# First step of an attention and two-MoE kernel: per-head scans of s, constant rows by GpSimd, two row loads for the fourth pair, idle matmuls on a constant tile

## The chip, the cores and the metric

The kernel runs on one core of a Trainium2 chip. The metric is the device time of one execution in microseconds (us); of several executions the median is given. A core has five engines with a queue each: TensorE (PE in the profile), VectorE (DVE), ScalarE (ACT), GpSimd (POOL) and SyncE (SP), which here issues DMAs. Each engine works its queue in order and waits on semaphores for the others.

## The reference

Causal attention with a bias from running sums of s, then two expert-like layers, all in one launch. Shapes: q, k, v of 4 batches, 8 heads, 576 positions, 64 dimensions; s of 4 x 8 x 576.

```python
scores = scale * np.matmul(q, k.transpose(0, 1, 3, 2))       # scale = 1/8
cum = np.cumsum(np.maximum(s, 0.0), axis=-1)
bias = -(cum[:, :, :, None] - cum[:, :, None, :])
scores = np.where(causal, -1e9, scores + np.minimum(bias, 0.0))
attn = softmax(scores); out = np.matmul(attn, v)
x = out as 2304 tokens x 512
h = np.maximum(np.maximum(x @ w1, x @ w2), x @ w3); x = h @ w_out        # d_ff 768
y = ((x @ w_a) * (x @ w_b)) @ w_out2                                     # d_ff 1536
```

## The kernel before, in words

Heads go in pairs: 4 batches by 4 pairs of two heads. The sums of s are never subtracted on a vector engine: they enter the scores through extra rows of the contraction. Where a pair's 64 rows of k and q end, two more rows hold a sum and a constant, so that the matmul adds cum of the key and takes off cum of the query; the factor 8 (the root of 64) in them cancels the scale. For most of the kernel these operands come ready-made from DRAM (tiles of 66 rows), with the sums written to DRAM first (`store_sums`, L194 on) and loaded back.

The first step is different, and the change lies in it alone. `lead_in()` (L1069) does the first 256 positions (Q0 = 256) of batch 0 for all four pairs p = 0 to 3 before the sums have been through DRAM. s is loaded with one partition for each pair of batch and pair (16 partitions), its columns being the two heads by 256 positions, and it is loaded four times, to partitions 64 to 127 (L173). Tiles `cum` and `sraw` hold the sums and s. A pair's operand tiles (`kraw` for p = 0, 1 and `kqv` for p = 2, 3, one tile for k and q) get k and q in partitions 0 to 63 by one DMA each (`lead_load`, L482). Partitions 64 to 127 are filled on the chip: k gets ones times a column of the identity in 64 to 95, which selects the row of pair p, and the sums times such a column in 96 to 127 (L1080, L1086); q gets the negative sums times 8 in 64 to 95 and the constant 8 in 96 to 127 (L1084, L1090). The scores of the first step are then matmuls with 128 rows of contraction (L1114), whose 64 upper rows are zero but for the pair's own.

Behind the scores of a head (`fs`, two matmuls of 128 and 256 columns) come the softmax in two parts: `sm_a` (L594), the masked minimum on VectorE (L608) and the exponential on ScalarE (L615), and `sm_b` (L621), the reciprocal on VectorE and the normalisation on GpSimd (L629). The normalised scores are transposed on TensorE (`ts`, L720), copied to SBUF by ScalarE or VectorE (L723) and multiplied with v (`pv`, L747), and the result is split into a high and a low part (Xh, Xl). The masked scores stand in tiles `F0` with the tag "P", of which there are four. `w_next` converts the first expert weights into high and low parts (hg and lg) between these steps; the gate matmuls (L813) use them.

Before the first scores, `spin` (L154) runs ten idle matmuls on the identity. A further one stands between the last pairs.

What sets the order: a scheduler puts each engine's instructions in a row by priority (`tc.high_priority`, higher first), by readiness and by `tc.issue_after`, which ties an instruction behind another. In `lead_in` the loads and idle matmuls have 5000, the rows of sums 4900, the loads of v and weights 4800, the rest 4000; the scan of s has 5100. SyncE issues nearly all loads in one queue: s, the four pairs' k and q, the tail of s, v, and then five weight loads of 512 KB.

## Time and profile before

| | |
|---|---|
| median of 3 runs | 882.74 us (882.62 to 883.32) |
| the profiled execution | 882.94 us |
| its span in the profile | 881.1 us |
| busy: TensorE, VectorE, ScalarE, GpSimd | 99%, 72%, 46%, 23% of the span |

The profile is one execution as the hardware's profiler recorded it. The times in its rows count from the start of the span, and the execution's own time has 1.84 us more around the span. Two records stand for one fp32 matmul of the program, so ten idle matmuls are 20 records. Busy shares are a mean over stages with different limits; what a change in one stage does is read from that stage's rows, and above all from what each engine waits for there. A row's last bracket gives the engine's idle time before the instruction and what ended it.

### The profile page before, as it was taken

The numbers are of one execution on the slowest core, as the hardware profiler recorded it, in microseconds if no ns is written. First come the engines' busy times: TensorE is split into PE (matmuls) and PEld (weight loads), VectorE is DVE, ScalarE is ACT, GpSimd is POOL, SyncE is SP. The second block draws the span as 40 slices with busy tenths as digits, with TensorE's granted clock in tenths as the row PEclk, the third lists the DMA queues.
The fourth block names the chain that finished last, engine by engine and source line by source line (L and its number), as shares of the span: only waits on it lengthen the run. The fifth ranks groups of instructions, "written<-read, shape, count | busy, mean of one in ns | idle before, by whom it ended". The sixth has DMA issues, their size and how long they took to land.

```text
span 881.1 us, 16779 instructions
## 1 busy us (share of the span) xinstructions
PE 869.9 (99%) x6024; PEld 828.0 (94%) x6024; DVE 633.9 (72%) x1437; ACT 402.0 (46%) x872; POOL 202.2 (23%) x316
## 2 busy tenths in 40 slices
PE   8999999999999999999999999999999999999998
PEld 6777999889999998999999999999999999999998
DVE  7986556675777666765797867777776859987873
ACT  7685745575656645554564323232322224433321
POOL 5324322233423323200003111111111310322210
PEclk9999999999999999999999999999999999999999
DMA  7665644265234763383302134444442353354331
GB/s 228 195 203 175 162 119 138 80 172 155 66 98 115 242 188 123 127 297 132 131 1 73 37 120 141 159 141 159 141 158 94 110 185 124 97 169 134 96 120 49
DMA packets 68291, 120.10 MB, mean 136 GB/s; under 512 B 6944, under 2 KB 50672, under 8 KB 68208
## 3 DMA queue, kind: packets, MB, share of 16 engines
q1 hardware_dynamic: 61016, 111.63, 39.9%
q10 hardware_dynamic: 7192, 7.40, 2.5%
q8 instruction: 48, 0.79, 0.4%
q14 instruction: 35, 0.29, 0.1%
HBM read 87.99 MB, written 31.01 MB: 135 GB/s over the span
## 4 chain that ended last, share of the span: by engine, by line
PE 94%; DMA 1%; DVE 1%; ACT 1%; issue 1%; POOL 1%; ACTq 0%; POOLq 0%; DVEq 0%
PE X L1270 29%; PE g L813 25%; PE Z L1270 15%; PE Y L1270 8%; PE fpv L747 5%; PE t L765 3%; PE f L681 2%; PE s L637 2%; PE s L638 2%; DMA wraw<-in_moe_w_dram 1%; PE ft L720 1%; PE W L1270 1%; PE sj L671 1%; PE tj L778 1%; PE sj L672 1%
## 5 line engine op out<-in xcount | busy, mean ns | idle before, releaser
L813 PE MATMUL g<-Xh,hg 128*128 128x256 f32 (+1 forms) x576 | 175.1, 307 | 1.3 <-ACT hg L81 0.6
L813 PE MATMUL g<-Xh,lg 128*128 128x256 f32 (+1 forms) x576 | 172.5, 301 | 0.3 <-DVE lg L92 0.3
L813 PE MATMUL g<-Xl,hg 128*128 128x256 f32 (+1 forms) x576 | 172.8, 301 | 0.0
L813 PEld LDWEIGHTS g<-Xh,hg 128*128 128x128 f32 x576 | 108.3, 189 | 5.6 <-ACT hg L81 1.2
L813 PEld LDWEIGHTS g<-Xh,lg 128*128 128x128 f32 x576 | 108.6, 189 | 3.0 <-DVE lg L92 1.3
L813 PEld LDWEIGHTS g<-Xl,hg 128*128 128x128 f32 x576 | 108.8, 189 | 1.8 <-issue 0.7
L88 POOL TENSOR_SCALAR wh<-wval 128x256 fp32r<-128x256 f32 x77 | 41.0, 542 | 273.4 <-DVE wval L346 224.2
L1270 PE MATMUL X<-xh,wh 128*128 128x384 f32 x288 | 97.2, 338 | 0.0
L1270 PE MATMUL X<-xl,wh 128*128 128x384 f32 x288 | 96.9, 336 | 0.0
L1270 PE MATMUL X<-xh,wl 128*128 128x384 f32 x288 | 96.9, 337 | 0.0
L1270 PE MATMUL X<-woh,slot 128*128 128x256 f32 x408 | 76.6, 281 | 0.5 <-ACT ob L1317 0.5
L629 POOL TENSOR_SCALAR P<-P,rs 128x128 f32<-128x128 f32 (+2 forms) x80 | 50.3, 634 | 96.2 <-DVE rs L625 70.2
L359 DVE TENSOR_TENSOR slot<-hraw,slot 128x768 fp32r<-128x768 f32 x60 | 60.9, 1041 | 13.7 <-POOL slot L88 11.0
L359 DVE TENSOR_TENSOR u<-Z,u 128x384 f32<-128x384 f32 x72 | 39.6, 552 | 37.9 <-ACT u L1317 28.2
L1270 PEld LDWEIGHTS X<-woh,slot 128*128 128x128 f32 x408 | 64.3, 189 | 0.7 <-ACT ob L1317 0.7
L615 ACT ACTIVATE P<-P,nm 128x128 f32<-128x128 f32 (+2 forms) x80 | 46.6, 583 | 34.6 <-DVE nm L608 26.1
L822 DVE TENSOR_TENSOR hf<-g,hf 128x256 f32<-128x256 f32 (+1 forms) x96 | 43.6, 454 | 24.7 <-PE g L813 18.6
L1270 PE MATMUL X<-wol,slot 128*128 128x256 f32 x204 | 56.9, 280 | 0.0
L81 ACT ACTIVATE slot<-hraw 128x768 fp32r<-128x768 f32 x39 | 32.5, 845 | 52.5 <-DVE hraw L359 25.9
L1270 PEld LDWEIGHTS X<-xh,wh 128*128 128x128 f32 x288 | 54.1, 188 | 0.5 <-DVE u L359 0.3
L1270 PEld LDWEIGHTS X<-xl,wh 128*128 128x128 f32 x288 | 54.1, 188 | 0.0
L1270 PEld LDWEIGHTS X<-xh,wl 128*128 128x128 f32 x288 | 54.0, 188 | 0.0
(214 smaller groups left out, 2208.8 us busy)
## 6 DMA issues: line engine op xcount, KB each, us to landing
hT<-u SPq DMA_DIRECT2D x72, 192.0 KB
hraw<-hT SPq DMA_DIRECT2D x36, 384.0 KB
wraw<-in_moe_w_dram SPq DMA_DIRECT2D x18, 512.0 KB
wraw<-in_moe_w_out_dram SPq DMA_DIRECT2D x18, 512.0 KB
kraw<-in_kT_dram SPq DMA_DIRECT2D x24, 288.0 KB
wraw<-in_moe_w_a_dram SPq DMA_DIRECT2D x12, 512.0 KB
wraw<-in_moe_w_b_dram SPq DMA_DIRECT2D x12, 512.0 KB
st<-h1T SPq DMA_DIRECT2D x24, 192.0 KB
```

What stands on the lines that cost most here:

```text
L81: return nc.scalar.activation(o, i, AF.Copy, scale=scale)
L88: nc.gpsimd.tensor_scalar(o, i, scale, 1.0, op0=ALU.mult, op1=ALU.mult)
L359: return {"V": nc.vector, "P": nc.gpsimd}[e].tensor_tensor(o, a, b, op=op)
L615: e_ = nc.scalar.activation(pt[:, c0:c1], pt[:, c0:c1], AF.Exp, bias=first, scale=-1.0, accum_out=sm[:, g : g + 1],)
L629: n_ = nc.gpsimd.tensor_scalar(pt[:, c0:c1], pt[:, c0:c1], rs[:, g : g + 1], 1.0, op0=ALU.mult, op1=ALU.mult,)
L637: nc.tensor.matmul(ps, QA1[:, qs], KB1[:, h, ksl], start=True, stop=False)
L638: nc.tensor.matmul(ps, QA2[:, qs], KB2[:, h, ksl], start=False, stop=True)
L747: e_ = nc.tensor.matmul(ps[h * D : h * D + D, c0:n], w, x, start=(t == 0), stop=(t == len(mm[h]) - 1),)
L765: nc.tensor.transpose(ps[:, j * P : j * P + P], pt[:, j * P : j * P + P], ident)
L813: nc.tensor.matmul(ps[:, :n], w[:, kk, :], x[:, kk, :], start=(i == 0), stop=(i == len(mm) - 1),)
L822: st["V"] = nc.vector.tensor_tensor(hf, ps[:, :n], hf, op=ALU.max)
L1270: e_ = nc.tensor.matmul(ps[:, :n], w, x, start=(first and i == 0), stop=(i == len(mm) - 1), skip_group_check=not first,)
```

## The change

- Scan: s is clipped and scanned by halves of 256 columns, one head each. VectorE clips the first half, ScalarE the second. The tile `reset`, which restarted the single scan at the second head, is gone. `scan_half(1)` is tied behind the first k sums of pair 0.
- Sums and constants: pair 0's rows of sums are made by halves. The constant rows of q for pairs 0 to 2 become memsets on GpSimd; the sums of k for pairs 1 and 2 and of q for pair 2 are GpSimd's, the sums of q for pairs 0 and 1 ScalarE's. A one-column exponential stands first on ScalarE.
- Fourth pair: no rows of 64 to 127. Two rows (64 and 65) of k and q are set to -8 and 8 by GpSimd and one of each is overwritten by a DMA from partition 67 of `cum`, and its matmuls contract over 66 rows.
- Idle matmuls: eleven, on a constant tile of ones, which exists before the kernel's own code. The identity gets the highest priority; the mask's tile is cleared by VectorE instead of GpSimd.
- Score tiles: both heads of the third pair use tag "sv", the first head of the fourth uses the tile that `reset` had; five heads share the four buffers of tag "P".

```diff
@@ -112,11 +112,12 @@
 
 
     ident = const.tile([P, P], F32, name="ident")
-    make_identity(nc, ident)
+    with tc.high_priority(5200):
+        make_identity(nc, ident)
 
     maskJ = const.tile([P, S // 2 + 4 * P], BF16, name="maskJ")
     mask = maskJ[:, S // 2 :]
-    nc.gpsimd.memset(maskJ, 0.0)
+    nc.vector.memset(maskJ, 0.0)
     nc.gpsimd.affine_select(
         out=mask[:, 3 * P :], in_=mask[:, 3 * P :], compare_op=ALU.is_ge, fill=NEG,
         base=0, pattern=[[-1, P]], channel_multiplier=1,
@@ -154,9 +155,10 @@
     def spin(n):
 
         ps = ps_m.tile([P, 512], F32, tag="m", name="spin")
+        one = nc.const_aps.tensor(1.0, [P, P], F32)
         for _ in range(n):
             last_pe[:] = [
-                nc.tensor.matmul(ps[:, :P], ident, ident, start=True, stop=True).ins
+                nc.tensor.matmul(ps[:, :P], one, one, start=True, stop=True).ins
             ]
 
     last_pe = [None]
@@ -167,18 +169,24 @@
         return ap_.tile([P, w], dt, tag=nm, bufs=1, name=f"e{nm}")
 
     cum, sraw = early("KB1"), early("KB2")
-    reset, ones = early("QA1")[:, : 2 * Q0], early("QA2")[:, : 2 * Q0]
+    ones = early("QA2")[:, : 2 * Q0]
     up, rr = slice(64, P), slice(64, 64 + SR)
+    halves = [slice(0, Q0), slice(Q0, 2 * Q0)]
     with tc.high_priority(5100):
         for a, e in enumerate((nc.sync, nc.scalar, nc.sync, nc.scalar)):
             e.dma_start(sraw[64 + a * SR : 64 + (a + 1) * SR, : 2 * Q0], s[:, : 2 * Q0])
-        nc.vector.memset(reset[up], 1.0)
-        nc.vector.memset(reset[up, Q0 : Q0 + 1], 0.0)
+        nc.scalar.activation(
+            ap_.tile([P, 1], F32, tag="small", bufs=10, name="warm"),
+            nc.const_aps.tensor(0.0, [P, 1], F32), AF.Exp,
+        )
         nc.vector.memset(ones[up], 1.0)
-        nc.vector.tensor_scalar_max(sraw[up, : 2 * Q0], sraw[up, : 2 * Q0], 0.0)
+        nc.vector.tensor_scalar_max(sraw[up, :Q0], sraw[up, :Q0], 0.0)
+        nc.scalar.activation(sraw[up, Q0 : 2 * Q0], sraw[up, Q0 : 2 * Q0], AF.Relu)
+
+    def scan_half(h):
+        c = halves[h]
         nc.vector.tensor_tensor_scan(
-            cum[up, : 2 * Q0], reset[up], sraw[up, : 2 * Q0], 0.0,
-            op0=ALU.mult, op1=ALU.add,
+            cum[up, c], ones[up, :Q0], sraw[up, c], 0.0, op0=ALU.mult, op1=ALU.add,
         )
 
     def scan_tails():
@@ -1071,29 +1079,52 @@
         LP = range(NP)
         with tc.high_priority(5000):
             lead = [lead_load(p) for p in LP]
-            spin(10)
+            spin(11)
         with tc.high_priority(4900):
             kk = [kn for kn, qn, vn in lead]
             qq = [qn for kn, qn, vn in lead]
             lo_, hi_r = slice(64, 96), slice(96, P)
-            for p in LP:
+
+            def k_sums(e, p, c):
+                return e.tensor_scalar(
+                    kk[p][hi_r, c], cum[hi_r, c], ident[hi_r, 96 + p : 97 + p], 1.0,
+                    op0=ALU.mult, op1=ALU.mult,
+                )
+
+            def q_sums(p, c):
+                nc.scalar.activation(
+                    qq[p][lo_, c], cum[lo_, c], AF.Copy, scale=-float(D) ** 0.5
+                )
+
+            for p in range(3):
                 (nc.vector if p < 2 else nc.gpsimd).tensor_scalar(
                     kk[p][lo_], ones[lo_], ident[lo_, 64 + p : 65 + p], 1.0,
                     op0=ALU.mult, op1=ALU.mult,
                 )
-                nc.scalar.activation(qq[p][hi_r], ones[hi_r], AF.Copy, scale=float(D) ** 0.5)
-            for p in LP:
-                (nc.vector if p < 2 else nc.gpsimd).tensor_scalar(
-                    kk[p][hi_r], cum[hi_r, : 2 * Q0], ident[hi_r, 96 + p : 97 + p], 1.0,
-                    op0=ALU.mult, op1=ALU.mult,
-                )
-                nc.scalar.activation(
-                    qq[p][lo_], cum[lo_, : 2 * Q0], AF.Copy, scale=-float(D) ** 0.5
-                )
+                nc.gpsimd.memset(qq[p][hi_r], float(D) ** 0.5)
+            nc.gpsimd.memset(kk[3][64:66], -float(D) ** 0.5)
+            nc.gpsimd.memset(qq[3][64:66], float(D) ** 0.5)
+            scan_half(0)
+            k_ = k_sums(nc.vector, 0, halves[0])
+            q_sums(0, halves[0])
+            with tc.issue_after(k_.ins):
+                scan_half(1)
+            k_sums(nc.vector, 0, halves[1])
+            q_sums(0, halves[1])
+            for p in (1, 2):
+                k_sums(nc.gpsimd, p, slice(0, 2 * Q0))
+            q_sums(1, slice(0, 2 * Q0))
+            nc.gpsimd.tensor_scalar(
+                qq[2][lo_], cum[lo_, : 2 * Q0], -float(D) ** 0.5, 1.0,
+                op0=ALU.mult, op1=ALU.mult,
+            )
         with tc.high_priority(4800):
             nc.sync.dma_start(sraw[rr, 2 * Q0 :], s[0:SR, 2 * Q0 :])
             for p in LP:
                 nc.sync.dma_start(lead[p][2], qv0[0, p][:, 2 * Q0 :])
+            row = cum[67:68, : 2 * Q0]
+            nc.sync.dma_start(kk[3][64:65], row)
+            nc.sync.dma_start(qq[3][65:66], row)
             for j in range(NL):
                 fetch_w1(w1_keys[j])
 
@@ -1107,13 +1138,19 @@
             for h in range(2):
                 pool, tag = (ps_m, "m") if h else (ps_s, "s")
                 ps = pool.tile([P, 512], F32, tag=tag, name="f0")
-                pt = ap_.tile([P, S], F32, tag="P", bufs=4, name="F0")
+                if p == 2:
+                    pt = ap_.tile([P, 5 * P], F32, tag="sv", bufs=2, name="F0")
+                elif (p, h) == (3, 0):
+                    pt = early("QA1")
+                else:
+                    pt = ap_.tile([P, S], F32, tag="P", bufs=4, name="F0")
                 for i in range(2):
                     o = ps[:, P * i : P * (2 * i + 1)]
+                    kr = P if p < 3 else 66
                     def mm(o=o, i=i):
                         last_pe[:] = [nc.tensor.matmul(
-                            o, two(qq[p])[:, h, i * P : i * P + P],
-                            two(kk[p])[:, h, 0 : P * (i + 1)], start=True, stop=True,
+                            o, two(qq[p])[:kr, h, i * P : i * P + P],
+                            two(kk[p])[:kr, h, 0 : P * (i + 1)], start=True, stop=True,
                         ).ins]
                     on_pe(mm)
                 pend.append(sm_a([[(ps[:, 0:P], 0)], [(ps[:, P : 3 * P], P)]], pt, SCALE))
```

What it does to the rows of two engines at the start, and to TensorE's at the end of the first step. First GpSimd, from its first instruction of the kernel to the first normalisation (kraw: pairs 0 and 1; kqv: pairs 2 and 3; eKB_115: the sums; eQA: the ones). Before:

```order
masks.py:197 MEMSET ident 128x128
L119 MEMSET maskJ 128x800
masks.py:199 ISA
masks.py:199 AFFINE_SELECT ident<-ident 128x128
L120 AFFINE_SELECT maskJ<-maskJ 128x128
L126 AFFINE_SELECT maskJ<-maskJ 64x64 x2
L1080 TENSOR_SCALAR kqv<-eQA_118,ident 32x512 x2
L1086 TENSOR_SCALAR kqv<-eKB_115,ident 32x512 x2
L629 TENSOR_SCALAR F_217<-F_217,rs 128x128
```

After, from behind the identity's memset and two constant rows of L1104 on:

```order
masks.py:199 ISA
masks.py:199 AFFINE_SELECT ident<-ident 128x128
L1104 MEMSET kraw 32x512
L1100 TENSOR_SCALAR kqv<-eQA_117,ident 32x512
L121 AFFINE_SELECT maskJ<-maskJ 128x128
L127 AFFINE_SELECT maskJ<-maskJ 64x64 x2
L1105 MEMSET kqv 2x512
L1106 MEMSET kqv 2x512
L1089 TENSOR_SCALAR kraw<-eKB_115,ident 32x512
L1089 TENSOR_SCALAR kqv<-eKB_115,ident 32x512
L1117 TENSOR_SCALAR kqv<-eKB_115 32x512
L637 TENSOR_SCALAR F_221<-F_221,rs 128x128
```

Constant rows (L1104), the setting of the fourth pair's rows (L1105, L1106) and the sums of pairs 1 and 2 (L1089, L1117) stand there now; the mask's clearing has left, and the constants and sums of the fourth pair too.

SyncE, from the tail of s to the first store of sums (eKB_116: s; wraw: the expert weights). Before:

```order
L1094 DMA eKB_116<-in_s_dram 16x640
L1096 DMA qvraw<-in_qv_dram 128x256 x2
L1096 DMA kqv<-in_qv_dram 128x256 x2
L247 DMA wraw<-in_moe_w_dram 128x1024 x5
L196 DMA ck<-eKB_115 32x1x256
L498 DMA kraw<-in_k_dram 64x1152
```

After:

```order
L1122 DMA eKB_116<-in_s_dram 16x640
L1124 DMA qvraw<-in_qv_dram 128x256 x2
L1124 DMA kqv<-in_qv_dram 128x256 x2
L1126 DMA kqv<-eKB_115 1x16x32
L1127 DMA kqv<-eKB_115 1x16x32
L255 DMA wraw<-in_moe_w_dram 128x1024 x5
L204 DMA ck<-eKB_115 32x1x256
L205 DMA ck<-eKB_115 32x1x320
```

The two row loads of the fourth pair have come between the loads of v (qvraw, kqv) and of the weights, and wait for the second scan half and GpSimd's memset of their rows.

TensorE, at the end of the first step, from the last product with v to the first gates (fj: joint scores of the last 64 positions of two heads; hg, lg: high and low part of the gate weights). Before:

```order
L747 MATMUL fpv<-PF,kqv 64x256 x2
L747 MATMUL fpv<-PF,kqv 64x128 x2
L681 MATMUL fj<-kraw,qvraw 64x288 x4
L813 MATMUL g<-Xh,hg_0_140 128x256
L813 MATMUL g<-Xl,hg_0_140 128x256
L813 MATMUL g<-Xh,lg_0_141 128x256
L813 MATMUL g<-Xh,hg_0_140 128x256
```

After:

```order
L755 MATMUL fpv<-PF,kqv 64x128 x2
L821 MATMUL g<-Xh,hg_0_139 128x256
L821 MATMUL g<-Xl,hg_0_139 128x256
L821 MATMUL g<-Xh,lg_0_140 128x256
L821 MATMUL g<-Xh,hg_0_139 128x256
L821 MATMUL g<-Xl,hg_0_139 128x256
L821 MATMUL g<-Xh,lg_0_140 128x256
L821 MATMUL g<-Xh,hg_0_139 128x256
L821 MATMUL g<-Xl,hg_0_139 128x256
L821 MATMUL g<-Xh,lg_0_140 128x256
L821 MATMUL g<-Xh,hg_0_139 128x256
L689 MATMUL fj<-kraw,qvraw 64x288 x4
```

The joint scores stood ahead of the first gate matmul; now ten gate matmuls stand ahead of them, three of which use lg.

## Rows read from the trace of the kernel before

**Rows 1.** The page, section 4: share of the chain that ended last, by engine.
```profile
PE 94%; DMA 1%; DVE 1%; ACT 1%; issue 1%; POOL 1%; ACTq 0%; POOLq 0%; DVEq 0%
```

**Rows 2.** Stretches (start:end, length, busy us and count by engine, PEclk, DMA).
```profile
10.00:13.00 3.00, 2.64 (x17) 1.90 (x15) 2.84 (x12) 2.20 (x10) 1.49 (x4) 1.00 1.02 404
...
25.00:30.00 5.00, 4.23 (x28) 3.31 (x27) 5.00 (x12) 1.41 (x3) 2.18 (x3) 1.00 0.58 192
...
60.00:80.00 20.00, 19.43 (x133) 14.28 (x132) 16.14 (x47) 14.23 (x31) 9.08 (x15) 1.00 0.66 196
...
100.00:200.00 100.00, 99.89 (x774) 93.93 (x773) 61.22 (x202) 59.72 (x155) 27.85 (x50) 1.00 0.50 141
```

**Rows 3.** The chain that ended last, first 30 us (start, length, what).
```profile
1.20 2.05 DMA eKB<-in_s_dram
...
3.37 0.60 DVE eKB L178
...
4.00 1.60 DVE eKB L179
...
5.62 1.14 ACT kraw L1090 x2
...
12.57 0.16 issue
...
12.73 0.88 DVE eKB L188
```

**Rows 4.** TensorE in order of time, first 14 us (start, length, what, idle before).
```profile
2.02 4.40 PE L159 MATMUL spin<-ident 128*128 128x128 f32 x20 [2.02 <-POOL ident masks.py:199]
...
6.30 2.89 PE L1114 MATMUL f<-kraw 128*128 128x128 f32 x16
```

**Rows 5.** Line L1114: waits of its weight loads (ns min/median/max, starts).
```profile
L1114 PEldq EVENT_SEMAPHORE  x5: 51/51/907, 5.2 to 11.4; - x5
```

**Rows 6.** VectorE in order of time, 16.5 to 21.5 us.
```profile
17.12 0.29 DVE L608 CUSTOM_DVE_ANT_0 F<-f,maskJ 128x128 f32<-128x128 f32 x1 [0.69 <-POOL F L629]
```

**Rows 7.** TensorE while its granted clock is lower: busy time of 16.3 to 19.6.
```profile
16.30:19.60 3.30, 3.30 (x18) 2.08 (x18) 1.96 (x10) 2.11 (x8) 2.17 (x6) 0.50 0.60 141
```

**Rows 8.** Lines L1080 and L1086 by shape (ns min/median/max, starts).
```profile
L1080 POOL TENSOR_SCALAR kqv<-eQA,ident x2: 685/766/847, 3.0 to 3.7; 32x512 f32<-32x512 f32 x2
...
L1086 DVE TENSOR_SCALAR kraw<-eKB,ident x2: 485/704/924, 5.6 to 6.0; 32x512 f32<-32x512 f32 x2
...
L1086 POOL TENSOR_SCALAR kqv<-eKB,ident x2: 862/888/913, 5.8 to 6.7; 32x512 f32<-32x512 f32 x2
```

**Rows 9.** GpSimd in order of time, first 14 us.
```profile
0.73 0.20 POOL masks.py:197 MEMSET ident<- 128x128 f32 x1 [0.29 <-POOLq L1891]
...
0.87 0.77 POOL L119 MEMSET maskJ<- 128x800 bf16 x1
...
2.16 0.85 POOL L126 TENSOR_SCALAR_AFFINE_SELECT maskJ<-maskJ 64x64 bf16<-64x64 bf16 x2
...
9.48 1.90 POOL L629 TENSOR_SCALAR F<-F,rs 128x128 f32<-128x128 f32 x4 [1.97 <-DVE rs L625]
```

**Rows 10.** TensorE's weight loads in order of time, first 14 us.
```profile
11.61 1.18 PEld L1114 LDWEIGHTS f<-kqv 128*128 128x128 f32 x8
```

**Rows 11.** TensorE in order of time 13 to 23 us.
```profile
15.59 0.96 PE L720 MATMUL ft<-ident,F 128*128 128x128 f32 x3 [0.85 <-POOL F L629]
...
16.48 1.55 PE L747 MATMUL fpv<-PF,qvraw 128*64 128x256 f32 x8
...
21.80 0.87 PE L747 MATMUL fpv<-PF,kqv 128*64 128x256 f32 x8
```

**Rows 12.** TensorE in order of time, 24 to 31 us.
```profile
27.21 0.91 PE L681 MATMUL f<-kraw,qvraw 66*128 66x384 f32 x2 [0.48 <-DVE nm L608]
```

**Rows 13.** SyncE's queue in order of time.
```profile
13.64 0.60 SPq L197 DMA_DIRECT2D ck<-eKB  x1
...
19.40 0.27 SPq L498 DMA_DIRECT2D kraw<-ck  x1
```

## The prediction

> **What bounds the kernel now.** I read the shares of the chain that ended last first: TensorE is 94% of it [rows 1]. Then the busy time by stretches: TensorE works 99.89 of 100 us from 100 to 200 us and 19.43 of 20 from 60 to 80, but 4.23 of 5 from 25 to 30, where VectorE works 5.00 of 5 [rows 2]. So the kernel is a TensorE kernel with a start of about 30 us in which other things set the pace, and the diff touches only that start. A microsecond won there moves the whole rest forward, because what follows has hardly a gap to lose it in: 0.57 us from 60 to 80 and 0.11 from 100 to 200.
>
> The start itself is read from the beginning of the chain [rows 3]: the load of s lands at 3.25 (1.20 + 2.05), VectorE clips it (0.60), scans both heads in one instruction (1.60), ScalarE then makes the scaled sums for four pairs (the first two take 1.14, all four up to 7.8) before its first exponential. TensorE meanwhile runs 20 records of idle matmuls from 2.02 to 6.42, starting when GpSimd has made the identity, and its first scores start at 6.30 [rows 4]. The operands of pair 0 that come by DMA are there at 5.2: at that time the weight load of the first scores has passed its first wait, the one on the DMA [rows 5]. So the first scores lose 1.1 us to sums and idle matmuls, not to the transfer. Later in the start, VectorE stands 0.69 us for a buffer that GpSimd still normalises [rows 6], and TensorE runs 3.3 us at the lower level of its clock, granted 0.50, which is 1.2 of 2.4 GHz [rows 7].
>
> **The change part by part.**
>
> Clip and scan by halves: the clip of 512 columns takes 0.60 and splits into two halves side by side on VectorE and ScalarE, 0.30 to 0.35 each. The scan of 512 columns takes 1.60, one half 0.80 [rows 3]. From 3.37: clip to 3.70, first scan half 3.72 to 4.52. Then pair 0's k sums of one head on VectorE, half of the 0.70 that 512 columns take [rows 8], and its q sums on ScalarE, half of 0.57 (1.14 for two) [rows 3] with some fixed part, 0.39. Both end at about 4.95. The second scan half, behind the k half on VectorE, ends at about 5.7. VectorE also gets the mask's clearing, 0.77 on GpSimd before [rows 9]; it stands ahead of 3.3, where VectorE waits for s anyway, so it costs nothing.
>
> ScalarE: four constant rows (four times 0.57) and five of eight half-units of q sums go away, and the table load is put ahead of the wait for s by a one-column exponential. That load was ahead of that wait before as well, so it brings nothing. ScalarE is free at 6.0 to 6.6 instead of 7.8.
>
> Idle matmuls: they need only a constant tile now, so they start when the queues start, about 0.8 [rows 9] instead of 2.02. Eleven are 22 records. At the price of now (4.40 for 20, [rows 4]) they end at 5.6. But the clock rises in between: the 16 first score records, eight of 128 and eight of 256 columns, take 2.89 us [rows 4]; at 0.22 for 128 columns, the idle matmuls' price, they would take 5.2. So the rise came at about 6.0, after some 4.0 us of idle matmuls. I take it to come as long after the first of them as now, at 4.8; then the last three or four records run at half price and end at about 5.2. First scores of pair 0 then start at 5.27, held by its DMA at 5.2: **−1.03 us**. VectorE and ScalarE, which follow at the same distance, are free by then (6.1 and 6.6, against a first maximum at about 6.3 and a first exponential at 6.8).
>
> GpSimd: it loses the mask's clearing (0.77) and takes three memsets of 32x512 and two of 2x512. A memset of 128 columns takes 0.20, one of 800 two-byte columns 0.77 [rows 9]; I take 0.5 for 512 columns, bounds 0.3 and 0.8. In its order: identity's memset, two memsets, identity's select (end 2.2), a memset, the constants of p 2 (0.77, [rows 8]) to 3.5, masks 0.25 and 0.85 [rows 9] to 4.6, two memsets to 5.6. Then sums: k of pair 1 when the second scan half is there at 5.7, to 6.6; k of pair 2 to 7.5; q of pair 2 to 8.3, at 0.89 each [rows 8]. Pair 1's scores need 6.6, and TensorE reaches them at about 6.7 behind two heads of 0.72. Pair 2's need 8.3. VectorE and ScalarE are then still on pair 1, whose last head is done with about 9.4 (four heads by 0.9 from 6.8 on), so both are covered. Its first normalisation, 9.48 now [rows 9], becomes possible at about 8.4, behind that 8.3. If the memsets cost 0.8, everything here comes 1.5 later, and pair 2's scores at 9.8 are some 0.4 past their cover; with the normalisations behind it I put up to 0.6 as a plus end.
>
> Buffers: pair 2's two heads and the first of pair 3 no longer share the four score buffers, so the wait of 0.69 for GpSimd [rows 6] goes. What is late next is the transposition that VectorE waited for 2 us later, and it moves along with its own inputs. I count all of it, **−0.69**, bounds 0 and −0.69. The two tail scans follow each other directly now, without the reciprocal between them, which leaves out an issue gap of 0.16 [rows 3]: **−0.16**.
>
> Pair 3's rows: two DMAs of one partition, from the sums to the operands, stand in SyncE's queue ahead of five weight loads. The first weight load goes out at about 9.0 rather than 6.7, but the DMA engines are busy throughout from 10 to 13 us (share 1.02, [rows 2]), and the weights are first touched past 20 us. So the loads land as before. The rows queue behind the v loads, which land at 10.6 by the DMAs' semaphores; I take 10.8. Pair 3's scores start at 11.6 now [rows 10], at 10.8 after. Cost 0; the bound is the fifth case.
>
> Sum: −1.03 − 0.69 − 0.16 = −1.88 against the profiled execution of 882.94 us (span 881.1, 1.84 around it), so 881.06. That execution lies 0.20 above the median of the three runs, 882.74, so against the median the time is **880.9**. Own range −1.2 to −2.7: buffers 0, or memsets at their upper price (−1.3); and on the other end the TensorE stretch at 1.2 GHz partly avoided.
>
> One row speaks against putting sums on GpSimd beside VectorE's scans. The tail scan of 320 columns takes 0.88 and the lead scan of 512 columns 1.60 [rows 3], so per column 2.7 and 3.1 ns; the second ran beside GpSimd's constants. That is at most 0.2 us longer for the whole scan, and VectorE's two k sums spread from 0.485 to 0.924 [rows 8]. The Trainium skill, page "SBUF — State Buffer", section "Who interferes with whom", states more: a VectorE instruction with two inputs in SBUF contends with a GpSimd instruction that reads SBUF, for a pair of ports that one of them holds for its whole instruction. By it the first scan half could wait for one mask select (0.43, half of 0.85), and the sum would be −1.45; the trace agrees that there is contention, but not with a full block. A wait of 0.43 there lies within the forecast's own range, in the part that counts as no change below.
>
> **The rivals.**
>
> B, the clock doesn't fall. TensorE stood for 0.85 us ahead of 15.59 and the stretch at 0.50 follows [rows 7, 11]. Eight records cost 1.55 in it and 0.87 outside [rows 11], so 3.3 us of work there would take 1.85: at most −1.45 more. With one buffer wait less and pair 3's scores ahead of time, TensorE may stand less before that point, and the fall may not come. Part of the gain would be covered by VectorE and ScalarE, so I take −1.0 beside the sum: 879.9. Against it: the normalisation on GpSimd that TensorE waited for is still there.
>
> C, the clock rises late. The idle matmuls start at 0.8, but the rise comes at about 6.0 as now. They end at 5.6 and the first heads run at 1.2 GHz, 1.44 each instead of 0.72 until 6.0. First scores at 5.6 and a slower first head leave about −0.3 of the first term: −0.3 − 0.69 − 0.16, so 881.6. For it: nothing in the trace shows that the rise follows the first matmul rather than a time of its own. The Trainium skill says on the page "TensorE: Matmul & The Clock Gate", section "What's actually happening", that the point of the rise differs from run to run of the same kernel; three runs within 0.7 us here show little of that.
>
> D, the order further on gives it back. The scheduler puts ten gate matmuls ahead of the joint scores that stood before them, and these gates wait for the weights' low part from VectorE, which has no idle time from 25 to 30 [rows 2]; TensorE already stands 0.48 there for VectorE [rows 12]. If the joint scores (1.14) no longer fill that wait, and the maximum behind them is late by as much, TensorE loses up to 0.77 + 1.14 = 1.9. All of it lost gives 882.8, the time before.
>
> E, slower: the rows land late. TensorE's queue is in order, and pair 3's scores stand in it ahead of the transpositions of pair 1, so all of it waits for the two small DMAs. Price: landing minus 10.8. A comparable transfer, the sums' store and reload, took 5.7 us from the store's issue to the reload's (13.64 to 19.40, [rows 13]) behind the weights. If the second row is issued at 7.9, behind pair 2's landing, that would be 13.6, a price of 2.8 and 883.7, slower than before. The gain is gone from a landing of 12.7 on, and the kernel is slower by over 0.2% from 14.5 on. Against it: the weights stand behind the rows in this queue, while that store stood behind the weights.
>
> **How the numbers follow.** Chances: forecast 0.42, B 0.22, C 0.16, D 0.08, E 0.12. About 0.2% (1.77 us) is what a measurement tells from no change, so faster means under 880.97 and slower over 884.51. The forecast is on that edge; its range is longer on the lower side, so 0.28 of its 0.42 count as faster, and with B's 0.22 that is 0.50. Same: 0.14 of the forecast, C 0.16, D 0.07, E 0.05, together 0.42. Slower: E 0.07, D 0.01 (a second wait of the same kind), together 0.08. The range leaves out half of B below 879.5 (it reaches to −1.45) and E above 883: 879.3 to 883.0.
>
> **What would show it.** Right: idle matmuls start before 1.0; first scores by 5.3 and the first exponential by 6.8; no VectorE wait on GpSimd near 15 to 17 us; pair 3's scores at about 10.8; the first gates about 1.9 us earlier. C shows as score records of 0.4 us in pair 0; B as no stretch with a granted clock of 0.50 between 12 and 20 us; D as TensorE waits on VectorE of over 1 us between 22 and 31; E as TensorE standing before pair 3's scores for a DMA. The prediction is wrong if the first scores move by 1 us and the end doesn't follow.

## The result, and the profile after

The kernel after takes 887.47 us (median of 5 runs, 885.0 to 888.81), the kernel before 882.74 beside it (882.01 to 883.32, 5 runs). The ratio is 1.0055, 95% interval 1.0045 to 1.0065: **slower by 4.7 us**, where 880.9 was forecast and 883.0 was the upper end of the range. The profiled execution is the one of 888.81 us (span 886.7), the slowest of the five, so its rows show the loss at its largest. Three executions of the experiments, far above all others (944 us in e3, 2201 in e10, 2867 in e12), are left out of the ratios below.

The page's shares of the chain that ended last [rows 1], of after. TensorE has lost three parts in a hundred, VectorE has gained three, DMA one:

```profile
PE 91%; DVE 4%; DMA 2%; issue 1%; ACT 1%; POOL 1%; ACTq 0%; DVEq 0%; POOLq 0%
```

Busy time by stretches, as in [rows 2, 7] (start:end, length, busy us and count of PE, PEld, DVE, ACT, POOL, then PEclk and DMA), of after:

```profile
25.00:30.00 5.00, 4.49 (x34) 3.38 (x32) 5.00 (x11) 1.64 (x4) 2.33 (x3) 1.00 0.69 220
...
60.00:80.00 20.00, 17.16 (x105) 12.18 (x104) 14.10 (x46) 13.46 (x30) 6.70 (x8) 0.91 0.55 174
100.00:200.00 100.00, 100.00 (x777) 92.97 (x777) 59.93 (x207) 59.87 (x155) 28.15 (x51) 1.00 0.46 134
16.30:19.60 3.30, 3.30 (x18) 2.07 (x20) 1.94 (x7) 2.00 (x8) 1.65 (x4) 0.50 0.94 304
```

From 25 to 30 TensorE works 4.49 us rather than 4.23, but it is 0.68 us behind by then: the eleventh gate matmul, which in both kernels has ten gates and the joint scores ahead of it, starts at 26.77 rather than 26.09. In this execution the granted clock is 0.50 from 14.6 to 21.4, before only from 16.3 to 19.6. From 100 us on TensorE is full again. Most of the loss lies from 55 to 80, which the diff doesn't touch: from 60 to 80 it is 17.16 of 20 busy rather than 19.43, at a mean granted clock of 0.91 rather than 1.00.

TensorE in order of time, first 14 us, of after, the rows that answer to [rows 4, 10] (start, length, what, idle before):

```profile
0.77 4.41 PE L161 MATMUL spin<-const-float32-1.0 128*128 128x128 f32 x22 [0.77 <-PEq L1928]
5.96 3.20 PE L1151 MATMUL f<-kraw 128*128 128x128 f32 x16 [0.78 <-DVE kraw L1089]
...
11.42 1.49 PE L1151 MATMUL f<-kqv 66*128 66x128 f32 x8
```

The first scores start at 5.96 instead of 6.30, a gain of 0.34, and behind idle matmuls that ended at 5.2 they stand 0.78 for VectorE's sums. The fourth pair's scores, at 11.42, wait for no DMA.

VectorE (first fence) and GpSimd (second) in order of time, of after:

```profile
2.38 1.66 DVE L1100 TENSOR_SCALAR kraw<-eQA,ident 32x512 f32<-32x512 f32 x2 [0.46 <-POOL ident masks.py:199]
3.96 0.37 DVE L183 TENSOR_SCALAR eKB<-eKB 64x256 f32<-64x256 f32 x1
4.36 0.69 DVE L188 TENSOR_TENSOR_SCAN eKB<-eQA,eKB 64x256 f32<-64x256 f32 x1
5.08 0.61 DVE L1089 TENSOR_SCALAR kraw<-eKB,ident 32x256 f32<-32x256 f32 x1
```

```profile
2.05 0.29 POOL masks.py:199 TENSOR_SCALAR_AFFINE_SELECT ident<-ident 128x128 f32<-128x128 f32 x1
2.40 0.52 POOL L1104 MEMSET kraw<- 32x512 f32 x1
3.02 0.73 POOL L1100 TENSOR_SCALAR kqv<-eQA,ident 32x512 f32<-32x512 f32 x1
```

The identity is ready at 2.34 (2.05 + 0.29), VectorE's two constant rows wait for it and take 0.83 each beside GpSimd's work, and so the clip starts at 3.96, not at 3.37 when s is there. In the kernel before, the same two rows took 0.44 each, beside mask selects on GpSimd:

```profile
2.04 0.87 DVE L1080 TENSOR_SCALAR kraw<-eQA,ident 32x512 f32<-32x512 f32 x2
```

Further on, the chain of after between 30 and 80 us leads through three loads of expert weights (start, length, what):

```profile
38.71 5.14 DMA wraw<-in_moe_w_dram
...
50.10 4.71 DMA wraw<-in_moe_w_dram
...
63.28 5.55 DMA wraw<-in_moe_w_dram
```

And TensorE stands for what is made from them (in order of time, 55 to 72 us, of after):

```profile
58.14 0.71 PE L689 MATMUL fj<-kraw,qvraw 66*64 66x288 f32 x4 [0.72 <-DVE hf L830]
...
60.90 0.39 PE L821 MATMUL g<-Xh,lg 128*128 128x256 f32 x1 [0.73 <-DVE lg L92]
...
70.21 0.39 PE L821 MATMUL g<-Xh,hg 128*128 128x256 f32 x1 [1.84 <-ACT hg L81]
```

Behind 25 us both kernels have the same instructions. What differs there is their order on the engines, which the scheduler makes anew for the whole program: up to about 100 us it is not the same in the two. So two theories stand against each other. **Start:** something in the changed first step costs the time. **Order:** the first step is harmless, and the new order of unchanged work behind it costs it.

### The profile page after: what moved, and what is told of

It is laid out like the page before. It is cut to its first block, busy times and chain, and to the rows that moved or that the text cites. A ratio compares the mean times of both kernels' runs of the same rounds, so it can differ in the third digit from the quotient of the medians.

```text
span 886.7 us, 16791 instructions
## 1 busy us (share of the span) xinstructions
PE 873.0 (98%) x6026; PEld 829.2 (94%) x6026; DVE 631.5 (71%) x1437; ACT 400.3 (45%) x869; POOL 204.3 (23%) x320
## 4 chain that ended last, share of the span: by engine, by line
PE 91%; DVE 4%; DMA 2%; issue 1%; ACT 1%; POOL 1%; ACTq 0%; DVEq 0%; POOLq 0%
PE X L1307 29%; PE g L821 23%; PE Z L1307 14%; PE Y L1307 8%; PE fpv L755 5%; PE t L773 2%; DMA wraw<-in_moe_w_dram 2%; PE s L645 2%; PE s L646 2%; PE ft L728 1%; PE W L1307 1%; PE f L689 1%; DVE wraw L270 1%; PE sj L679 1%; PE tj L786 1%
## 5 line engine op out<-in xcount | busy, mean ns | idle before, releaser
L821 PE MATMUL g<-Xh,hg 128*128 128x320 f32 (+1 forms) x576 | 174.4, 306 | 2.1 <-ACT hg L81 1.8
L821 PE MATMUL g<-Xl,hg 128*128 128x320 f32 (+1 forms) x576 | 172.4, 300 | 0.0
L367 DVE TENSOR_TENSOR slot<-hraw,slot 128x768 fp32r<-128x768 f32 x60 | 60.4, 1032 | 13.8 <-POOL slot L88 11.0
```

Of the source, the lines that this page charges most:

```text
L367: return {"V": nc.vector, "P": nc.gpsimd}[e].tensor_tensor(o, a, b, op=op)
L821: nc.tensor.matmul(ps[:, :n], w[:, kk, :], x[:, kk, :], start=(i == 0), stop=(i == len(mm) - 1),)
```

## The experiments

The kernel before ran beside every experiment; the ratio is to it, with its 95% interval (it is not the quotient of the two medians). In the diffs "..." marks lines left out.

| | median us | before | ratio |
|---|---|---|---|
| e1 after, order of before | 883.29 | 882.67 | 1.0010 (1.0001 to 1.0019) |
| e2 before, order of after | 885.88 | 882.67 | 1.0036 (1.0023 to 1.0048) |
| e3 e1, identity and masks first | 882.38 | 882.79 | 0.9998 (0.9989 to 1.0006) |
| e4 e1, four score buffers again | 883.41 | 882.79 | 1.0005 (0.9996 to 1.0013) |
| e5 e1, idle matmuls at 14 us | 882.56 | 882.79 | 0.9998 (0.9989 to 1.0006) |
| e6 e3 and e5 | 882.35 | 882.79 | 0.9993 (0.9985 to 1.0002) |
| e7 after, order of before up to 39 us | 885.99 | 882.58 | 1.0050 (1.0033 to 1.0066) |
| e8 after, order of before from 39 us on | 884.33 | 882.58 | 1.0022 (1.0012 to 1.0032) |
| e9 e3, two weight loads later | 882.05 | 882.58 | 0.9999 (0.9990 to 1.0008) |
| e10 e6, two weight loads later | 881.06 | 882.58 | 0.9985 (0.9977 to 0.9994) |
| e11 before, additions of e10 | 881.73 | 882.60 | 0.9993 (0.9982 to 1.0004) |
| e12 e10 again | 881.60 | 882.60 | 0.9988 (0.9979 to 0.9997) |

### e1 and e2: the order exchanged

Each engine's instructions from the first scores on are tied in a row, by edges that only set the order and add no wait. The table ORDER holds the order of the other kernel. e1 is after with the order of before, e2 is before with the order of after. So "order" takes in the softmax, transpositions and products of the first step itself; what stands ahead of the first scores (first loads, scans by heads, constants, rows of sums) stays each kernel's own.

```diff
+    for runs in ORDER:
+        row = [behind[k] for a, n in runs for k in range(a, a + n)]
+        for x, y in zip(row, row[1:]):
+            tc.add_manual_dep(
+                y, x.name,
+                mybir.DependencyInfo(
+                    mybir.DependencyClass.NoSync, mybir.DependencyReason.DATA
+                ),
+                reason="order",
+            )
```

> The changed kernel whole, but everything behind the first step's scores is put on each engine in the order of the kernel before (a table of rows, tied by order alone, no waits added). Theory 1, the loss is the order that the scheduler made behind the first step: both kernels stand at the same place at 25 us (last Xl of the first step 24.98 after, 25.01 before), so the time is that of before, 882.7, within 0.6. Theory 2, the loss is in the lead-in itself (the longer stretch of 1.2 GHz, the row loads, the later weights): 886 to 888 as the changed kernel.

> The kernel before whole, with the changed kernel's order behind the first step's scores. Theory 1: 885 to 888, with TensorE waits for converted weights between 57 and 71 us of about 3 us together. Theory 2: 882.7 as before, since the lead-in is that of before.

With the order of before, the changed kernel takes 883.29: of the 4.7 us, 4.2 (887.47 - 883.29) are gone, and 0.6 is left (883.29 - 882.67; by the interval 0.1 to 1.7). The unchanged kernel with the order of after takes 3.2 us more (885.88 - 882.67), which leaves 1.5 of the 4.7. So by the medians the order costs 3.2 to 4.2 us, and the start, with whatever the ties themselves cost (no run shows that alone), 0.6 to 1.5. As the main cause the start falls.

Where it costs, by stretches, first after, then e1 (columns as above):

```profile
55.00:60.00 5.00, 4.10 (x31) 2.93 (x29) 4.94 (x11) 3.52 (x9) 0.00 (x0) 1.00 0.68 172
60.00:66.00 6.00, 5.27 (x41) 4.84 (x40) 4.53 (x18) 4.13 (x10) 1.81 (x2) 1.00 0.71 205
66.00:72.00 6.00, 3.89 (x16) 1.78 (x16) 3.77 (x13) 3.91 (x9) 2.05 (x2) 1.00 0.41 156
72.00:80.00 8.00, 8.00 (x52) 5.57 (x51) 5.80 (x19) 5.42 (x13) 2.84 (x4) 0.79 0.54 164
```

```profile
55.00:60.00 5.00, 4.84 (x36) 3.83 (x36) 5.00 (x15) 3.93 (x10) 0.25 (x1) 1.00 0.82 235
60.00:66.00 6.00, 6.00 (x36) 3.87 (x36) 4.92 (x16) 4.02 (x9) 1.79 (x3) 1.00 0.76 228
66.00:72.00 6.00, 6.00 (x44) 4.32 (x45) 5.42 (x15) 4.75 (x11) 2.34 (x2) 1.00 0.66 198
72.00:80.00 8.00, 8.00 (x61) 6.55 (x61) 6.20 (x20) 5.43 (x14) 5.38 (x11) 1.00 0.62 178
```

From 55 to 72 us TensorE is idle 3.58 us longer in after (0.74 + 0.73 + 2.11), and from 72 to 80 the lower clock costs another 1.7 (8.00 times 0.21). Together 5.3, against 5.7 between the two spans (886.7 and 881.0). In e2 the waits are partly others: 1.02 us before 58.58 for a load of q, then 0.65 for `lg` before 61.16, and none at 70. The clock falls between the two, for longer than in after:

```profile
60.00:66.00 6.00, 5.34 (x23) 4.84 (x23) 4.57 (x15) 3.92 (x10) 1.82 (x2) 0.54 0.74 209
```

**How the order does it.** Weights come through three staging buffers. A load may be issued only when the low part (`lg`) of the block three before it has been made from the same buffer; it then takes some 5 us, the conversion follows, and the gate matmuls wait for it. It is a loop of load, convert, free, load. Loads and blocks are counted from 0 here, as in the expectations of e7 and e8. Load 8 waits for block 5's `lg`. VectorE first in after, then in e1:

```profile
36.49 0.69 DVE L270 SCALAR_TENSOR_TENSOR wraw<-wraw 128x512 int32<-128x512 int32 x1
...
37.17 0.67 DVE L616 CUSTOM_DVE_ANT_0 F<-f,maskJ 128x512 f32<-128x512 f32 x1
...
37.77 1.51 DVE L92 TENSOR_TENSOR lg<-wraw,hg 128x512 fp32r<-128x512 f32 x2
```

```profile
36.34 0.69 DVE L92 TENSOR_TENSOR lg<-wraw,hg 128x512 fp32r<-128x512 f32 x1
36.95 0.99 DVE L270 SCALAR_TENSOR_TENSOR wraw<-wraw 128x512 int32<-128x512 int32 x1
```

In after, another block's conversion and a masked minimum stand ahead of `lg`; in e1 `lg` stands first. The load in SyncE's queue, after and then e1:

```profile
38.71 0.33 SPq L255 DMA_DIRECT2D wraw<-in_moe_w_dram  x1
```

```profile
37.06 0.33 SPq L255 DMA_DIRECT2D wraw<-in_moe_w_dram  x1
```

It goes out 1.65 us later. Three loads on, each waiting for the one three before, load 11 goes out at 48.70 rather than 47.12, load 14 at 60.87 rather than 58.37, load 17 at 71.89 rather than 68.54. By these rows alone, most could come from the swap at 36 us.

TensorE's longest wait, 1.84 us at 70, doesn't fit that, though. It waits for block 14's `hg`, and in ScalarE's queue this stands behind the first conversion of the next block, which waits for load 15 (ScalarE in order of time, of after):

```profile
68.91 0.68 ACT L266 ACTIVATE wraw<-wraw 128x512 f32<-128x512 f32 x1 [2.09 <-DMA wraw<-in_moe_w_dram]
69.50 0.65 ACT L81 ACTIVATE hg<-wraw 128x512 fp32r<-128x512 f32 x1
```

Load 15 belongs to the series 9, 12, 15. It goes out at 63.28 (59.75 in e1) and load 12 at 50.10 (48.67), but load 9 isn't late: 39.31, and 39.40 in e1. What delays this series begins behind load 9.

### e7 and e8: at which place the order costs

Theory: load 8's delay is all there is, and the rest follows from it. Rival: the order behind 39 us makes delays of its own. Each kernel takes one order up to about 39 us and the other behind it; the diff, against e1, is one of the rows of the table that change.

```diff
-        (212, 1), (543, 10), (567, 10), (584, 12), (218, 1), (230, 4), (247, 1), (603, 2),
+        (212, 1), (543, 10), (567, 10), (584, 12), (218, 1), (230, 4), (247, 1), (241, 4),
```

> The changed kernel, its later rows in the order of before up to about 39 us and in its own order behind that. Theory D, the loss starts before 39 us: the low part of the weight block 5 (lg at 37.77, 36.34 with the order of before) frees its buffer late, so load 8 goes out at 38.71 rather than 37.06, and loads 11, 14 and 17, each three further on, inherit it: load 8 back at 37.1, and of the 4.2 us between e1 and the changed kernel 1.6 or more regained, 885.9 or less. Rival: the order behind 39 us makes the loss by itself: 887.

> The other half: the changed kernel in its own order up to about 39 us, and in the order of before behind that. Theory D, the late load 8 is inherited whatever the order behind it: loads 8, 11, 14, 17 later than in e1 by 1.5 each, 884.5 to 885. Rival: 883.3 as e1.

e7 brings load 8 back to 37.33 and takes 885.99 all the same, an interval that covers that of after. SyncE's queue in e7, loads 14 and 17:

```profile
60.54 0.37 SPq L255 DMA_DIRECT2D wraw<-in_moe_w_dram  x1
...
70.33 0.35 SPq L255 DMA_DIRECT2D wraw<-in_moe_w_dram  x1
```

In e1 they go out at 58.37 and 68.54, in after at 60.87 and 71.89. So the delay isn't handed down from load 8 alone: the order behind 39 us makes it too, 2.7 us of the 4.2 by itself (885.99 - 883.29; by the ratios, 1.0050 and 1.0010, it would be 3.5). That it acts through the loop of buffers fits the rows; no run changes the loop alone. e8 lies 1.0 above e1 (884.33 and 883.29, intervals that overlap). Its profiled execution, with 881.74 the shortest of its twelve, has no stretch at the lower clock behind the first scores. Its last product with v starts at 21.38, where after with the same rows up to there has 23.24, and load 8 goes out at 37.06 although VectorE has the order of after (`lg` at 36.12). So the 1.65 us of load 8 in after's profile aren't the order alone; the longer stretch at the lower clock in that execution is in them. What e8's 1.0 consists of stays open.

### e3: the late identity

To e1 one edit is added: GpSimd makes the identity and the masks first, and its own and VectorE's constant rows come behind the masks.

```diff
-    nc.vector.memset(maskJ, 0.0)
+    with tc.high_priority(5200):
+        nc.vector.memset(maskJ, 0.0)
...
+            with tc.issue_after(masked):
+                for p in range(3):
+                    (nc.vector if p < 2 else nc.gpsimd).tensor_scalar(
```

> As e1 (the changed kernel with the later order of before), but GpSimd makes the identity and the masks first and sets constant rows after them, so that VectorE's two constant rows (L1100, 1.66 us for two, from 2.39) run from about 1.9 beside mask selects, as in the kernel before (0.87 for two). Theory A, VectorE's constant rows were slowed by GpSimd's memsets and by the late identity and hold the clip: rows done by 2.9, clip at 3.4 rather than 3.97, first scores at 5.3 rather than 5.97. Whether it reaches the end: theory B, it does not, since the TensorE stretch at 1.2 GHz takes it up: within 0.4 of e1 (883.3); its rival, it passes on whole: 882.6.

TensorE, VectorE and GpSimd of e3, in order of time, each in its own fence:

```profile
5.54 3.19 PE L1158 MATMUL f<-kraw 128*128 128x128 f32 x16 [0.72 <-DVE kraw L1095]
```

```profile
2.05 1.23 DVE L1107 TENSOR_SCALAR kraw<-eQA,ident 32x512 f32<-32x512 f32 x2
3.43 0.47 DVE L189 TENSOR_SCALAR eKB<-eKB 64x256 f32<-64x256 f32 x1 [0.15 <-DMA eKB<-in_s_dram]
```

```profile
2.18 0.81 POOL L1111 MEMSET kraw<- 32x512 f32 x1
```

The clip starts at 3.43 and waits for s alone, the first scores start at 5.54: 0.42 more is won than in after. The median falls 0.9 under e1, near the rival's 882.6, but the intervals overlap, and 0.9 is more than was won. e3's profiled execution also has no stretch at the lower clock in the first step (its fall comes from 44.4 to 48.0), so what the earlier identity brings at the end isn't shown. The constant rows are still long (0.62 each), and now GpSimd's memset beside them is too: 0.81, where in after it kept its 0.52 and VectorE's rows took 0.83.

### e4: the buffer wait

To e1 one edit is added: all eight heads use the four score buffers of before.

```diff
-                if p == 2:
-                    pt = ap_.tile([P, 5 * P], F32, tag="sv", bufs=2, name="F0")
-                elif (p, h) == (3, 0):
-                    pt = early("QA1")
-                else:
-                    pt = ap_.tile([P, S], F32, tag="P", bufs=4, name="F0")
+                pt = ap_.tile([P, S], F32, tag="P", bufs=4, name="F0")
```

> As e1, but all eight heads of the first step use the four score buffers of before. By the prediction's sum the buffer wait is worth 0.69 us, so 884.0. By the traces of before and after it is worth nothing, since TensorE at 1.2 GHz and not VectorE sets the pace there: 883.3 as e1, with VectorE's wait for GpSimd of some 0.7 us back near 16 to 17 us and the same first gate, 24.6.

VectorE's wait of [rows 6] is back in e4:

```profile
16.77 0.29 DVE L616 CUSTOM_DVE_ANT_0 F<-f,maskJ 128x128 f32<-128x128 f32 x1 [0.61 <-POOL F L637]
```

But TensorE's first gate starts no later, in e4 (first fence) than in e1 (second), and the medians lie 0.12 apart (883.41 and 883.29):

```profile
24.55 0.39 PE L821 MATMUL g<-Xh,hg 128*128 128x256 f32 x1
```

```profile
24.64 0.39 PE L821 MATMUL g<-Xh,hg 128*128 128x256 f32 x1
```

The intervals are too wide to rule out 0.69 us by the time alone, but the first gate shows that the wait is lost before 25 us: it lies where TensorE, at half clock in both executions (0.50 from 16.6 to 19.8 us in e4), sets the pace. What it would be worth where the clock stays up wasn't run.

### e5 and e6: the clock in the first step

Four idle matmuls, into unused columns, stand ahead of each of the second pair's two groups of transpositions, where TensorE stands idle and its clock falls afterwards. Both are added to e1; e6 has the edits of e3 and e5.

```diff
-    def f_t0(PF, h, pt, lead=False):
+    def f_t0(PF, h, pt, lead=False, idle=0):
...
+        one = nc.const_aps.tensor(1.0, [P, P], F32)
+        for _ in range(idle):
+            idles.add(nc.tensor.matmul(ps[:, 3 * P :], one, one, start=True, stop=True).ins.name)
```

> As e1, with four idle matmuls ahead of each of the two groups of transpositions of the second pair, where TensorE stands 0.64 and 0.86 us for the normalisation. Theory C, the stretch at 1.2 GHz is what takes up the lead-in's gain: granted clock 1.0 from 13 to 20 us, the first gate at 23.3 rather than 24.6, and the time 1.0 lower than e1, 882.3. Rival: the stretch is covered by VectorE's and ScalarE's work, or comes anyway: 883.3 as e1, or 0.3 above for the idle matmuls.

> e3 and e5 together. Theory A and C: 881.4 to 881.8, under the kernel before by 0.9 to 1.3 us, first scores at 5.3 and first gate at about 22.6. Rival: as e5.

The clock stays up in e5 in the stretch of [rows 7], and TensorE then stands elsewhere:

```profile
16.30:19.60 3.30, 2.89 (x26) 1.74 (x24) 2.64 (x13) 2.70 (x10) 2.30 (x7) 1.00 1.03 294
```

```profile
24.60 1.19 PE L689 MATMUL fj<-kraw,qvraw 66*64 66x288 f32 x8 [2.08 <-DMA qvraw<-cq]
```

The next limit is the reload of the sums for the joint scores, 2.08 us in e5 and 2.46 in e6, which start later than in e1 (23.57). In these two executions the fall isn't avoided but moved: behind that wait the granted clock is 0.50 from 26.4 to 29.4 in e5 and from 26.8 to 29.8 in e6. Over all runs the idle matmuls bring 0.7 by the medians (883.29 and 882.56), inside the intervals. The profiled execution of e5 is one of its slower ones (883.52): in 7 of 11 the mean granted clock over the whole execution is 1.000, and their median is 882.20.

### e9 to e12: the reload earlier

The last two of the first five weight loads go behind the stores of the sums in SyncE's queue, so that stores and reload come sooner. e9 has it beside e3, e10 beside e6; e11 is the kernel before with the idle matmuls and the later loads; e12 is e10 again.

```diff
+            stored = tc.nc.cur_bb.bb.instructions[-1]
+            for i in loads[3:]:
+                tc.add_manual_dep(
+                    i, stored.name,
...
+                    reason="behind the sums",
```

> As e3, with the last two of the five first weight loads behind the stores of the sums in SyncE's queue. In e3 and e5 TensorE stood 1.32 and 2.08 us before the joint scores near 23 us for the sums' reload (qvraw<-cq), whose stores were queued behind the weights. Theory E, that reload is what is late next: the wait goes, the joint scores start near 21.7 and the time is 1 us under e3, 881.4. Rival: the weights or VectorE's conversions (busy from 20 to 31 us) take it up: as e3, 882.4.

> As e9, with the idle matmuls of e6. Theory E: no wait for qvraw<-cq, granted clock 1.0 from 13 to 25 us, 881.2 and less spread from run to run than e9. Rival: 882.4 as e6.

> The kernel before with its own order and lead-in, and the two additions of e10: four idle matmuls ahead of each of the second pair's groups of transpositions, and the last two of the first five weight loads behind the stores of the sums. Theory F, e10's 1.5 us come from these two and not from the changed lead-in: 881.1 as e10. Theory G, the lead-in's earlier scores are needed too: 881.9 to 882.3, about 0.5 under before.

> e10 once more, beside e11. If e10's gain over the kernel before is real, 881.1 within 0.5 and a ratio under 1 with its whole interval; if it was one draw among runs that differ by 2 us, 882.4 as e6.

In e9 the joint scores have no wait, but the clock is low in the first step (0.53 from 16.3 to 19.6), and nothing beyond the intervals is won over e3:

```profile
23.20 1.17 PE L695 MATMUL fj<-kraw,qvraw 66*64 66x288 f32 x8
```

e10 and e12 are the only versions under the kernel before by more than their interval, by 1.5 and 1.0 us. In the profiled execution of e10 the wait is there nevertheless, for a load of q that stands in SyncE's queue behind the two moved loads; TensorE first, then SyncE:

```profile
24.57 1.19 PE L695 MATMUL fj<-kraw,qvraw 66*64 66x288 f32 x8 [2.80 <-DMA qvraw<-in_q_dram]
```

```profile
14.34 4.40 SPq L261 DMA_DIRECT2D wraw<-in_moe_w_dram  x2
18.84 0.75 SPq L512 DMA_DIRECT2D qvraw<-in_q_dram  x1
```

In e12 the same wait is 1.21 us, in e11 there is none. So the moved loads brought a wait of their own, and through which rows the 1 us of e10 is won isn't shown. The profiled execution of e10 (882.50, a fall behind that wait) isn't the usual one: 7 of the 10 in the ratio have a mean granted clock of 1.000 and a median of 880.84, the other three 0.997 and 882.09. The clock alone isn't it either, for of the 106 executions of the kernel before beside the experiments, the 28 with 1.000 have a median of 882.66 and the 56 with 0.998 one of 882.72. e11, without any of the original change, comes to 881.73 beside e12's 881.60: the two aren't told apart, so no gain of the changed first step is shown even in the best version.

## Why the prediction was wrong, step by step

**First scores, -1.03: the mechanism right, the size a third.** The measured gain is 0.34. The idle matmuls ended at 5.2 as forecast, and they weren't the limit. The failed term is "first scan half 3.72 to 4.52": it let VectorE's constant rows stand ahead of s for nothing, as they did before. They start 0.34 later (2.38 and 2.04), since two GpSimd constants of 0.52 stand ahead of the identity's select, and last 0.79 longer for both (1.66 and 0.87). Before, VectorE stood 0.46 for s behind them; that cover is used up, and the clip comes 0.59 late besides (3.96 and 3.37). The prediction listed the order of GpSimd with the select's end at 2.2, and didn't ask who waits for it. e3 undid it and got 0.42 of the 0.69 back. The other 0.27 is about what pair 0's first k sums took more than counted: 0.61 in after and 0.63 in e3, not 0.35.

The constant rows have one input and still got longer beside GpSimd's memset and constants. The Trainium skill, page "SBUF — State Buffer", section "Who interferes with whom", says that `tensor_scalar` may use both pairs of ports and then contends with GpSimd, and that the second of the two stands until the first is done. The traces agree that there is contention, and that it can fall on either side (VectorE's row from 0.44 to 0.83 in after, GpSimd's memset from 0.52 to 0.81 in e3); neither row shows a stand as long as the other's whole instruction. The two-input scan of 256 columns, for which the prediction had feared it, took 0.69 in every trace that has it.

**Buffers, -0.69: wrong.** In e4 the first gate is no later with the wait. VectorE's wait was counted because it was there; what waited for VectorE at that time was a TensorE at half clock that had enough to do. [Rows 7] had said so.

**Tail scans, -0.16: as said.** The two stand directly behind each other in after (1.65 for both), but no gain from it can be seen behind 16 us; that the half clock covers it too is argued, not tried.

**GpSimd and the rows of the fourth pair, 0: right.** No wait on GpSimd's sums, none on the two small DMAs (11.42, no DMA named): rival E didn't happen. The fourth pair's scores come at 11.42, though, not at the forecast 10.8; in TensorE's queue they stand behind a transposition at 11.14 that waits for GpSimd's normalisation. The first weight load, out at 9.0 as forecast, costs nothing either.

**The sum carried forward: the step that failed most.** "A microsecond won there moves the whole rest forward" holds only if the rest stays as it is. The sum promised 1.88 us at the end; even with the old order (e1), the first gate starts at 24.64 rather than 24.79 and the time isn't better. And the rest didn't stay. That is rival D's mechanism, the order further on, and D got 0.08 and a price of 1.9 at most, since it was priced at 25 to 31 us, where the first difference shows. There TensorE in fact works more than before. The price, 3.2 to 4.2 us by e2 and e1, came mostly at 55 to 80 us, where TensorE waits for late weights and the clock falls behind these waits. [Rows 2] with TensorE idle 0.57 us of 20 from 60 to 80 was read as "hardly a gap to lose it in"; the chain of before, read in [rows 3] for its first 30 us only, says otherwise of that stretch:

```profile
60.17 5.79 DMA wraw<-in_moe_w_dram
68.98 5.21 DMA wraw<-in_moe_w_dram
```

Two weight loads fill 11 of its 20 us. TensorE is full there, but these loads stand in the chain that ended last, so there was little room for them to come later.

**B and C, the clock.** The fall that B took away came: in after's profile from 14.6 to 21.4, in e1's from 15.9 to 19.3. In those of e3, e8, e11 and e12 it doesn't come in the first step at all, in e3 and e8 without the added idle matmuls. C's late rise is there too, but not in each: the page's clock column reads 1.00 in this stretch throughout, so the rise is read from the records, which take 421 ns at first and 273 behind it. The same 22 idle records, started at 0.77, took 4.41 us in after, and in e1 (no short record among them) and e3

```profile
0.77 5.02 PE L161 MATMUL spin<-const-float32-1.0 128*128 128x128 f32 x22 [0.77 <-PEq L2023]
```

```profile
0.77 4.06 PE L167 MATMUL spin<-const-float32-1.0 128*128 128x128 f32 x22 [0.77 <-PEq L2030]
```

So "as long after the first of them as now" was no rule. The Trainium skill, page "TensorE: Matmul & The Clock Gate", section "What's actually happening", states that the point of the rise differs between runs of one kernel; these rows, of three kernels with the same idle matmuls, fit that. C costs nothing here: in e1 the idle matmuls end 0.6 later than in after, and the first scores start at 5.97 as against 5.96. B doesn't decide either: in the kernel before, executions with a mean clock of 1.000 are no faster (882.66 and 882.72, above). In after's own profile the long fall does delay the end of the first step, by 1.86 us against e8's.

**The end of the range.** 883.0 left out D with a price of more than the gain, since its loss was bounded by one wait seen before. Several late loads, each with its own wait, and a fall of the clock behind them, aren't held by that bound.

## What to carry to other kernels

Where a scheduler orders the whole program, a local edit is two edits: its own, and a new order of everything behind. Freeze the order of the unchanged part to see the one without the other, and before a forecast compare the two orders for as far as they differ, above all around instructions that free a buffer for a load, and around those that stand in a queue behind the first use of one. A wait is worth something only if what it holds up is itself late, so ask of each wait that goes which engine sets the pace at that moment.

## What the runs showed of the hardware

- A wait of TensorE can be paid for a second time, in the clock. In after, waits of 0.73 and 1.84 us for converted weights are followed by a granted clock of 0.50 from 72.6 to 76.0; in e2, waits of 1.02 us for q and 0.65 for weights by one from 60.4 to 67.2; in e5, e6 and e10, waits of 2.08, 2.46 and 2.80 us by one from about 26.5 to 29.5. It isn't so each time: behind e7's waits of 0.53 to 0.63 us near 60 and 68 the clock stays at 1.00.
- A fall needn't cost anything at the end: executions of the kernel before with a mean granted clock of 1.000 (28) and of 0.998 (56) have medians of 882.66 and 882.72. Where there is more of it, the time is longer: in e8 the seven executions with 0.998 or more took 881.74 to 884.52, the five with 0.996 or less 883.64 to 887.00. Which of the two brings the other isn't shown.
- The five runs of after spread from 885.0 to 888.8, those of the kernel before beside them from 882.0 to 883.3, but its 106 executions beside the experiments from 880.84 to 884.57. So five runs don't show that one spreads more than the other.
- Constant rows on VectorE and memsets on GpSimd, which share no data, are longer beside each other: VectorE's 0.83 us in after rather than 0.44 beside mask selects, GpSimd's 0.81 in e3 rather than 0.52.
